# A planner that treats the ports shared by VectorE and GpSimd as an exclusive lock, in a decay-attention and MoE kernel

## The chip, the cores and the metric

The kernel runs on one core of a Trainium2 chip. The core has five engines, each working through its own instructions in a fixed order: TensorE (PE, matmuls), VectorE (DVE), ScalarE (ACT), GpSimd (POOL) and SyncE (SP, which here issues all DMAs). An instruction waits at the head of its engine's queue until what it needs is done, and what stands behind it waits as well. The metric is the device time of one execution in microseconds (us), as the median over several runs.

## The reference

Eight batches of eight heads, 576 positions, head size 64, all in float32. The causal attention has a decay from the running sum of log f, and its output, with the heads side by side, goes through two matmuls with a piecewise function between them.

```python
def _attn_ref(q, k, v, f):
    B, H, S, D = q.shape                                  # 8, 8, 576, 64
    scores = np.matmul(q, k.transpose(0, 1, 3, 2)) / np.sqrt(D)
    cum = np.cumsum(np.log(np.clip(f, 0.0001, 1.0)), axis=-1)
    decay = cum[:, :, :, None] - cum[:, :, None, :]
    scores = np.where(causal, -1000000000.0, scores + decay)
    attn = np.exp(scores - np.max(scores, axis=-1, keepdims=True))
    attn = attn / (np.sum(attn, axis=-1, keepdims=True) + 1e-09)
    return np.matmul(attn, v)

def _moe_ref(x, w_in, w_out):                             # x: 4608 x 512
    h = x @ w_in                                          # 512 x 2048
    g = np.where(h >= 1, h, np.where(h <= -1, 0.0, (h + 1) ** 2 / 4))
    return g @ w_out                                      # 2048 x 512
```

## The kernel before

**The work.** Two heads make a pair; 36 jobs (`jobs`, the first batch is cut into rows 0 to 255 and the rest) run over the pairs. A job has row blocks of 128 rows. For each block, `scores` puts the scores into PSUM with PE (L831), POOL makes the decay row in SBUF (tensor_scalar, L837, and the causal affine_select, L841), and `weights` lets DVE subtract the two with the row minimum on the way (L923, one input in PSUM, one in SBUF), ACT take the exponential and its sum (L927), and DVE the reciprocal (L935, L938). From the sixth job on, float32 values are carried as two float16 parts: ACT writes the high part (L941), DVE the rest as value minus high part (scalar_tensor_tensor with both tensors in SBUF, L947; for some blocks of two jobs POOL does it, L945), and a transposing DMA puts them the other way round (L953). The first five jobs stay in float32 and are transposed by PE against a diagonal that ACT writes (`turn_rows`, L852, L863). `values` multiplies with V (L968, results by L977 and L978). `prepare` splits and transposes Q and K of the next job (L745, L747, one buffer `qs`; in the first twelve jobs they stay in float32 and PE transposes them, L709 to L718), `measure` takes their norms, `split_values` splits V (L794, L795), `value_max` reads V for its largest value (L544). Decay rows lie in a ring of four buffers (`sdr`) and one of two (`sd4`).

**The MoE.** Tokens are taken in chunks of 256 and the hidden columns in eight blocks of 256; one chunk with one block is a unit. `moe_front` multiplies into the PSUM tile `ph` (two buffers, L1012), ACT writes relu(u) and its square (L1021, L1022), DVE chooses between them (L1023, one input in PSUM), ACT writes the high half of g (L1025) and DVE the low half (L1026, both inputs in SBUF). `moe_back`, two units later, multiplies g with the second weights (L1041) and empties the sums (L1054, L1058). The weights, too, are split into two float16 parts at the beginning, by `weight_split`: three integer steps on DVE (L495, L498, L501), squares on ACT (L505), a scale (`from_norms`, L409 to L418), the high part on ACT (L509), and the low part on POOL (L511, L512) or DVE (L514). `moe_scales` derives each batch's small factors (L579 to L604).

**The order.** The program is first written in one order. Then `plan` (the last line of the kernel) rearranges it: `traced` makes a `Step` of every instruction, with what it must follow, a duration from `Step.cost` (times `SLOW`, except on PE) and a rank, which is its place in the program plus `SHIFT` for the function and engine that it comes from. `arranged` then plays the steps through in time. For each engine it takes, among the steps that are ready, one that can begin within `LOOK` = 50 ns of the engine's becoming free, the lowest rank first, and otherwise the one that can begin first; the engine whose choice begins earliest goes next. It models rings of buffers, DMA queues, a PE clock that halves after a quiet window, and the overlap of successive instructions. The order found is pinned on every engine. The hardware keeps that order and takes its own time. In `arranged` before, DVE and POOL know nothing of each other but their data.

The constants before:

```python
SLOW = 1.03
LOOK = 50
SHIFT = {("from_norms", "PE"): -100, ("measure", "DVE"): 400, ("moe_back", "DVE"): 200,
         ("moe_back", "SP"): 800, ("split_values", "ACT"): 1500, ("turn_rows", "ACT"): -25,
         ("value_max", "DVE"): -100, ("weight_split", "DVE"): 200, ("weights", "POOL"): 400}
```

Of the kernel before, what the change touches and what calls it, by code (L numbers as in the profile page):

```python
# [49 lines left out]
RING = 1500  # L50
SLOW = 1.03
LOOK = 50
SHIFT = {
    ("from_norms", "PE"): -100,
    ("measure", "DVE"): 400,
    ("moe_back", "DVE"): 200,
    ("moe_back", "SP"): 800,
    ("split_values", "ACT"): 1500,
    ("turn_rows", "ACT"): -25,
    ("value_max", "DVE"): -100,  # L60
    ("weight_split", "DVE"): 200,
    ("weights", "POOL"): 400,
}

# [27 lines left out]
class Step:  # L92


    def __init__(self, k, ins):
        self.k, self.ins, self.engine = k, ins, ENGINES[ins.engine.name]
        self.reads, self.writes = ([self.part(a) for a in args if hasattr(a, "bass_ap")] for args in (ins.ins, ins.outs))
        self.after, self.waits, self.tiles = set(), [], set()

    @staticmethod  # L100
# [17 lines left out]
    def cost(self):  # L118
        e, out = self.engine, self.writes[0]
        n = out[4]  # L120
# [11 lines left out]
        if e == "ACT":  # L132
            return 150 + (0.82 if wide and wide[0][0][:2] in ("s_", "ph", "po") else 0.93) * n + 100 * min(len(self.reads) - 1 + len(self.writes) - 1, 3)
        if e == "POOL":
            if self.ins.opcode == "TensorTensor":
                return 450 + 2.0 * n
            return 260 + 0.95 * n if "Affine" in self.ins.opcode else 460 + 1.15 * n
        if wide:
            n = max(n, wide[0][4])
        fast = len(wide) == 1 and self.ins.opcode == "TensorScalarPtr"  # L140
        return 170 + 55 * (scalars > 0) + (0.6 if fast else 1.08) * n + (20 if len(self.writes) > 1 else 0)

# [66 lines left out]
def arranged(steps, users, order, rings):  # L209
# [15 lines left out]
    ready = {e: {} for e in LATE}  # L225
    chains = {e: [] for e in LATE}
    fly, dma, warm, border, busy, form = [], 0.0, False, WINDOW, 0.0, None
    for s in steps:
        if not s.open:
            ready[s.engine][s.k] = 0  # L230
    for _ in steps:
        best = None
        for e, cands in ready.items():
            pick = None
            for k, t in cands.items():
# [10 lines left out]
                else:  # L246
                    begin = max(t, free[e])
                    c = (free[e] if begin <= free[e] + LOOK else begin, s.rank, begin, k)
                    if pick is None or c < pick:
# [45 lines left out]
        else:  # L295
            end = t + s.time
            free[e] = end - OVERLAP[e]
        s.end = end + LATE[e]
# [923 lines left out]
```

## Time and profile before

| | |
|---|---|
| median of 3 runs | 1062.35 us (1059.92 to 1063.02) |
| the profiled execution, its own time | 1060.71 us |
| its span, first to last instruction | 1058.9 us |
| mean granted PE clock | 0.973 |
| busy: PE, DVE, ACT, POOL | 1003.1, 793.0, 786.9, 435.4 us |
| packets' time of the DMA queue, share of 16 engines' span | 61.0% |

Busy time is the union of an engine's instructions. A DVE or POOL instruction that has been started and stands still counts as busy. The granted clock is 1 when PE runs at its full clock. A line such as L1026 is a line of the kernel file; names such as g<-u,z say what is written from what.

### The profile page before, as it was taken

To read this page: it belongs to the slowest core of one execution; us is meant where nothing else is said; L and a number is where in the kernel's file an instruction comes from. 1 tells how busy PE (TensorE), PEld (TensorE's weight loads), DVE (VectorE), ACT (ScalarE), POOL (GpSimd) and SP (SyncE) were. 2 spreads that over 40 slices of the span, in tenths; PEclk is the share of its full clock that TensorE was granted. 3 is DMA by queue.
4 is the path that set the end of the run, shared out by engine and by line. 5 is a ranking of instruction groups with operands and counts; after the bars stand their busy time and mean duration, and the time that the engine had idled before them with its cause. 6 is when DMAs were issued, how large, how long until landed. Compare 5 with 4: busy or idle time off the path is not lost.

```text
span 1058.9 us, 24420 instructions
## 1 busy us (share of the span) xinstructions
PE 1003.1 (95%) x8859; PEld 657.7 (62%) x8859; DVE 793.0 (75%) x2095; ACT 786.9 (74%) x1634; POOL 435.4 (41%) x677
## 2 busy tenths in 40 slices
PE   3769888799999999999999999999999999999998
PEld 2546555366666676667666666666666666677665
DVE  5999999999998878977776677887788866322222
ACT  3788888788888878886776688888888877344443
POOL 2887776736443544442332344454445441000000
PEclk9869899889999999999999999999999999999999
DMA  9967669789997777785455476767676654000000
GB/s 298 305 203 206 167 163 194 182 169 187 198 189 184 175 167 151 170 185 128 119 128 131 81 175 144 158 150 160 147 161 143 142 104 95 3 22 19 3 20 20
DMA packets 406041, 152.18 MB, mean 144 GB/s; under 512 B 379680, under 2 KB 382752, under 8 KB 405920
## 3 DMA queue, kind: packets, MB, share of 16 engines
q1 hardware_dynamic: 405920, 150.62, 61.0%
q8 instruction: 69, 1.13, 0.5%
q14 instruction: 52, 0.43, 0.1%
HBM read 75.64 MB, written 9.58 MB: 80 GB/s over the span
## 4 chain that ended last, share of the span: by engine, by line
PE 56%; DMA 0%; DVE 0%; issue 0%; ACT 0%; DVEq 0%
PE ph L1012 25%; PE po L1041 24%; PE s L831 4%; PE s L968 3%; DMA vst<-in_v_dram 0%; DVE pr L947 0%; PE ph L409 0%; DVE u L1023 0%; PE ph L401 0%; DVE x L978 0%; ACT ot L1058 0%; PE ph L397 0%; ACT u L1022 0%; DVE sdr L923 0%; DVE rc L938 0%
## 5 line engine op out<-in xcount | busy, mean ns | idle before, releaser
L1012 PE MATMUL ph<-x,place 128*128 128x256 f16 (+3 forms) x4608 | 413.1, 247 | 1.2 <-DVE u L1023 0.7
L1041 PE MATMUL po<-place,g 128*128 128x512 f16 x1728 | 403.5, 381 | 2.3 <-ACT g L1025 1.0
L1012 PEld LDWEIGHTS <-place 128*128 128x128 f16 x4608 | 353.2, 99 | 61.9 <-issue 21.3
L1041 PEld LDWEIGHTS <-g 128*128 128x128 f16 x1728 | 165.9, 98 | 180.6 <-issue 8.0
L837 POOL TENSOR_SCALAR sdr<-ck,nsig,cqs 128x128 f32<-128x128 f32 (+1 forms) x192 | 150.1, 789 | 269.3 <-DVE pr L947 258.1
L1023 DVE SCALAR_TENSOR_TENSOR u<-ph,z,u 128x512 f32<-128x512 f32 x128 | 95.6, 747 | 128.5 <-ACT u L1022 128.3
L1021 ACT ACTIVATE u<-ph,z 128x512 f32<-128x512 f32 x128 | 98.8, 772 | 117.3 <-PE ph L1012 116.9
L927 ACT ACTIVATE sdr<-sdr,nm 128x384 f32<-128x384 f32 (+1 forms) x248 | 137.3, 555 | 24.7 <-DVE nm L923 22.2
L947 DVE SCALAR_TENSOR_TENSOR pr<-sdr,rc,pr 128x384 f16<-128x384 f32 (+2 forms) x232 | 126.7, 584 | 8.0 <-ACT pr L941 6.6
L1025 ACT ACTIVATE g<-u,z 128x512 f16<-128x512 f32 x128 | 91.8, 717 | 51.7 <-DVE u L1023 50.9
L1026 DVE SCALAR_TENSOR_TENSOR g<-u,z,g 128x512 f16<-128x512 f32 x128 | 98.2, 767 | 41.0 <-ACT g L1025 40.5
L941 ACT ACTIVATE pr<-sdr,rc 128x384 f16<-128x384 f32 (+1 forms) x236 | 118.7, 556 | 7.3 <-issue 2.8
L831 PE MATMUL s<-qkT 64*64 64x512 f16 (+11 forms) x1056 | 111.4, 336 | 6.0 <-DVE nm L923 2.9
L923 DVE CUSTOM_DVE_ANT_0 sdr<-s,sdr,nalpha 128x128 f32<-128x128 f32 (+1 forms) x192 | 99.0, 544 | 13.1 <-PE s L831 7.4
L841 POOL TENSOR_SCALAR_AFFINE_SELECT sdr<-sdr 128x128 f32<-128x128 f32 x248 | 97.7, 414 | 2.3
L837 POOL TENSOR_SCALAR sd<-ck,nsig,cqs 64x576 f32<-64x576 f32 x48 | 51.1, 1064 | 115.1 <-DMA ck<-cum_d 46.7
L1022 ACT ACTIVATE u<-u 128x512 f32<-128x512 f32 x144 | 89.7, 623 | 1.9
L968 PE MATMUL s<-pT,vs 128*64 128x320 f16 (+3 forms) x1098 | 69.8, 279 | 3.2 <-DVE nm L923 3.2
L968 PEld LDWEIGHTS <-vs 128*64 128x64 f16 x1098 | 48.6, 110 | 27.0 <-issue 9.3
L831 PEld LDWEIGHTS <-qkT 64*128 64x128 f16 (+1 forms) x864 | 32.4, 98 | 44.0 <-issue 29.4
L747 DVE SCALAR_TENSOR_TENSOR qs<-qk,sc,qs 128x640 f16<-128x640 f32 x48 | 45.6, 962 | 5.3 <-ACT qs L745 4.4
L837 POOL TENSOR_SCALAR sdr<-ck,cq 128x384 f32<-128x384 f32 (+3 forms) x48 | 40.4, 842 | 17.1 <-DVE pr L947 12.6
(157 smaller groups left out, 1027.7 us busy)
## 6 DMA issues: line engine op xcount, KB each, us to landing
ck<-cum_d SPq DMA_DIRECT2D x64, 288.0 KB, 4.0
out_dram<-ot SPq DMA_DIRECT2D x36, 256.0 KB, 2.2
qk<-in_k_dram SPq DMA_DIRECT2D x68, 128.0 KB, 2.7
vst<-in_v_dram SPq DMA_DIRECT2D x28, 288.0 KB, 3.4
v<-in_v_dram SPq DMA_DIRECT2D x62, 128.0 KB, 2.8
qk<-in_q_dram SPq DMA_DIRECT2D x60, 128.0 KB, 2.9
place<-in_moe_w_in_dram SPq DMA_DIRECT2D x6, 1024.0 KB, 6.9
place<-in_moe_w_out_dram SPq DMA_DIRECT2D x5, 1024.0 KB, 7.8
```

The costliest lines, as they stand in the source:

```text
L831: nc.tensor.matmul(sds[h % len(sds)][1][p0:p1, c0:c1], lhsT=a[rows, q0 - w.s0:q0 - w.s0 + p1 - p0], rhs=b[rows, c0:c1], start=(i == 0), st ...
L837: nc.gpsimd.tensor_scalar(out=sd[p0:p1, 0:wid], in0=w.ck[h][p0:p1, 0:wid], scalar1=w.nsig if w.p < NQK else w.nsig[p0:p1], scalar2=w.cqs[p ...
L841: nc.gpsimd.affine_select(sd[p0:p1, q0:wid], sd[p0:p1, q0:wid], pattern=[[-1, wid - q0]], channel_multiplier=1, base=0, compare_op=ALU.is_ ...
L923: nc.vector.tensor_tensor_reduce(out=a, in0=sp[:, 0:wid], in1=a, scale=w.nalpha, scalar=BIG, op0=ALU.add, op1=ALU.min, accum_out=nm[:, i:i ...
L927: nc.scalar.activation(a, a, AF.Exp, bias=nm[:, i:i + 1], scale=-1.0, accum_out=sm[:, i:i + 1])
L941: nc.scalar.activation(pr[:, :, 0, i, :], a, AF.Copy, scale=rc[:, i:i + 1])
L947: nc.vector.scalar_tensor_tensor(out=pr[:, :, 1, i, :], in0=a, scalar=rc[:, i:i + 1], in1=pr[:, :, 0, i, :], op0=ALU.mult, op1=ALU.subtract,)
L968: nc.tensor.matmul(av[64 * h:64 * h + 64, at + s0:at + s1], lhsT=w.vs[:, vl, h, t, :], rhs=w.pT[:, t, pl, h, s0:s1], start=(t == 0 and pi ...
L1012: nc.tensor.matmul(ph[:, fi, a0:a1], lhsT=wi[fb][:, wl, t, fi * P:(fi + 1) * P], rhs=xs[b][:, t, xl, s0:s0 + a1 - a0], start=(fi == 0 and ...
L1021: nc.scalar.activation(u, h, AF.Relu, scale=z.u[:, i:i + 1], bias=z.h[:, i:i + 1])
L1026: nc.vector.scalar_tensor_tensor(out=g[:, 1], in0=u, scalar=z.r[:, i:i + 1], in1=g[:, 0], op0=ALU.mult, op1=ALU.subtract)
L1041: nc.tensor.matmul(po[ch][i], lhsT=g[:, gl, fi * TC + i * P:fi * TC + (i + 1) * P], rhs=wo[fb][:, wl, fi, :], start=(first and fi == 0 and ...
```

## The change

Only the planner changes; the instructions and their data are the same, and their order on the engines is what it finds.

- `Step` has a new mark `shares`: DVE instructions of the kinds tensor_scalar, scalar_tensor_tensor and tensor_tensor that write more than one element per partition and whose first input isn't one of the PSUM tiles (`s_`, `ph`, `po`).
- `arranged` keeps `hold`, the end of the last such DVE step, and `pool`, the end of the last POOL step. A sharing DVE step may not begin earlier than `pool` - 140 ns, a POOL step not earlier than `hold` - 100 ns, and if one still begins ahead of that end, its own end is moved behind it.
- The formulas for durations of ACT, POOL and DVE steps get new constants, ACT no longer tells PSUM inputs from SBUF ones, and `SLOW` goes from 1.03 to 1.01.
- `SHIFT` is a new table: ("turn_rows", "ACT") and ("moe_back", "DVE") leave it, eight entries come in, and that of ("value_max", "DVE") is changed.

```diff
@@ -48,18 +48,26 @@
 ENGINES = {"PE": "PE", "DVE": "DVE", "Activation": "ACT", "Pool": "POOL", "SP": "SP"}
 WINDOW = 3413.3
 RING = 1500
-SLOW = 1.03
+SLOW = 1.01
+AWARE = True
 LOOK = 50
 SHIFT = {
+    ("across", "PE"): 50,
+    ("from_norms", "DVE"): -25,
     ("from_norms", "PE"): -100,
     ("measure", "DVE"): 400,
-    ("moe_back", "DVE"): 200,
+    ("moe_back", "ACT"): -1500,
     ("moe_back", "SP"): 800,
+    ("moe_front", "ACT"): -1500,
+    ("moe_scales", "DVE"): 25,
+    ("prepare", "DVE"): -1500,
     ("split_values", "ACT"): 1500,
-    ("turn_rows", "ACT"): -25,
-    ("value_max", "DVE"): -100,
+    ("turn_rows", "PE"): 50,
+    ("value_max", "DVE"): -25,
     ("weight_split", "DVE"): 200,
+    ("weights", "DVE"): 25,
     ("weights", "POOL"): 400,
+    ("weights", "SP"): 50,
 }
 
 
@@ -96,6 +104,10 @@
         self.k, self.ins, self.engine = k, ins, ENGINES[ins.engine.name]
         self.reads, self.writes = ([self.part(a) for a in args if hasattr(a, "bass_ap")] for args in (ins.ins, ins.outs))
         self.after, self.waits, self.tiles = set(), [], set()
+        self.shares = (
+            self.engine == "DVE" and ins.opcode in ("TensorScalarPtr", "TensorTensor")
+            and self.writes[0][4] > 1 and self.reads[0][0][:2] not in ("s_", "ph", "po")
+        )
 
     @staticmethod
     def part(a):
@@ -130,15 +142,15 @@
                 return max(1340, 1.17 * n)
             return 430 if n > 500 else 620
         if e == "ACT":
-            return 150 + (0.82 if wide and wide[0][0][:2] in ("s_", "ph", "po") else 0.93) * n + 100 * min(len(self.reads) - 1 + len(self.writes) - 1, 3)
+            return 190 + 0.845 * n + 92 * min(len(self.reads) - 1 + len(self.writes) - 1, 3)
         if e == "POOL":
             if self.ins.opcode == "TensorTensor":
-                return 450 + 2.0 * n
-            return 260 + 0.95 * n if "Affine" in self.ins.opcode else 460 + 1.15 * n
+                return 185 + 1.89 * n
+            return 177 + 0.86 * n if "Affine" in self.ins.opcode else 322 + 0.83 * n
         if wide:
             n = max(n, wide[0][4])
         fast = len(wide) == 1 and self.ins.opcode == "TensorScalarPtr"
-        return 170 + 55 * (scalars > 0) + (0.6 if fast else 1.08) * n + (20 if len(self.writes) > 1 else 0)
+        return 147 + 62 * (scalars > 0) + (0.52 if fast else 1.04) * n
 
 
 def clash(a, b):
@@ -224,6 +236,7 @@
     free = {e: 400 for e in LATE}
     ready = {e: {} for e in LATE}
     chains = {e: [] for e in LATE}
+    hold = pool = 0
     fly, dma, warm, border, busy, form = [], 0.0, False, WINDOW, 0.0, None
     for s in steps:
         if not s.open:
@@ -245,6 +258,10 @@
                         t = max(t, gone[queue[base][j]])
                 else:
                     begin = max(t, free[e])
+                    if AWARE and s.shares:
+                        begin = max(begin, pool - 140)
+                    elif AWARE and e == "POOL":
+                        begin = max(begin, hold - 100)
                     c = (free[e] if begin <= free[e] + LOOK else begin, s.rank, begin, k)
                     if pick is None or c < pick:
                         pick = c
@@ -294,6 +311,14 @@
             free[e] = end
         else:
             end = t + s.time
+            if e == "POOL":
+                if hold > t:
+                    end = max(end, hold + s.time - 100)
+                pool = end
+            elif s.shares:
+                if pool > t:
+                    end = max(end, pool + max(s.time - 140, 24))
+                hold = end
             free[e] = end - OVERLAP[e]
         s.end = end + LATE[e]
         for name in s.tiles:
```

## The prediction

> **What bounds the kernel now.** I read the page first, then the busy times by stretch, then PE's waits, then the groups of VectorE (DVE) in the stretch that the first views pointed to.
>
> ```profile
> PE 1003.1 (95%) x8859; PEld 657.7 (62%) x8859; DVE 793.0 (75%) x2095; ACT 786.9 (74%) x1634; POOL 435.4 (41%) x677
> PE   3769888799999999999999999999999999999998
> DVE  5999999999998878977776677887788866322222
> POOL 2887776736443544442332344454445441000000
> PEclk9869899889999999999999999999999999999999
> ```
>
> PE is busy 95% of the span, yet its first eight or nine slices are not full, and in just those DVE reads 9 in every slice but the first and POOL reads 7 to 8 in most. From the tenth slice on (about 240 us) PE is full to the end. The busy times by stretch give the sizes; the columns are the stretch, its length, then busy time of PE, PEld, DVE, ACT and POOL, the granted PE clock, the DMA share and GB/s.
>
> ```profile
> 0.00:80.00 80.00, 46.09 (x255) 33.49 (x256) 64.25 (x146) 49.89 (x114) 52.33 (x72) 0.81 0.85 269
> 80.00:106.00 26.00, 25.95 (x186) 15.61 (x186) 24.72 (x56) 22.50 (x45) 20.09 (x25) 0.98 0.75 203
> 106.00:159.00 53.00, 46.48 (x328) 28.16 (x325) 51.42 (x128) 46.23 (x93) 40.32 (x50) 0.94 0.68 165
> 159.00:212.00 53.00, 43.62 (x287) 22.40 (x285) 50.26 (x149) 42.84 (x97) 37.08 (x52) 0.90 0.86 187
> 212.00:240.00 28.00, 26.42 (x200) 17.04 (x201) 25.48 (x79) 24.27 (x52) 10.03 (x17) 0.88 0.86 177
> 240.00:901.00 661.00, 660.28 (x6358) 435.70 (x6356) 533.30 (x1485) 535.76 (x1143) 275.57 (x466) 1.00 0.69 151
> 901.00:1058.90 157.90, 154.24 (x1260) 105.28 (x1260) 43.57 (x58) 65.46 (x94) 0.00 (x0) 1.00 0.04 14
> ```
>
> From 240 to 901 us PE is idle 0.72 us at full clock, after that 3.66 us, which is the tail behind the last matmul. No order of the same work can win there; a poor one can lose. PE's idle time lies ahead of it: 80.00 - 46.09 = 33.9 us in the first 80 us, then 0.05 + 6.52 + 9.38 + 1.58 = 17.5 us up to 240 us. The clock is the second loss: the granted share below 1, times the stretch, is 15.2 us before 80 us and 26 x 0.02 + 53 x 0.06 + 53 x 0.10 + 28 x 0.12 = 12.4 us from 80 to 240 us, both upper bounds, since a slow clock costs nothing while PE idles. So the prize is at most 30 us between 80 and 240 us, and at most 49 us before it. As PE is full from 240 us on, a microsecond won ahead of it is a microsecond off the end.
>
> Who holds PE up there? PE's waits, in total us, times and the longest; the first row is from 0 to 80 us, the others from 80 to 240 us.
>
> ```profile
> PE ph L863 <- ACT pr L852: 22.7, 8, 9.5
> ...
> PE s L714 <- DVE rc L935: 3.3, 1, 3.3
> PE s L968 <- DVE nm L923: 3.2, 2, 1.7
> PE s L831 <- DVE nm L923: 2.9, 3, 1.5
> ...
> PE po L1041 <- ACT g L1025: 1.0, 1, 1.0
> PE po L1041 <- DVE g L1026: 0.9, 2, 0.5
> ```
>
> Early on PE waits for the diagonals of the first pairs (L852), which stand behind the chain of decay (POOL), subtraction (DVE) and exponential (ACT); later mostly for DVE. From 80 to 212 us DVE is busy 24.72 + 51.42 + 50.26 = 126.4 of 132 us, 96%, ACT 111.6, 85%. DVE is the nearest bound. But part of its busy time is waiting. The timelines of DVE (first two rows) and of POOL (last two) around 171 us, start, duration, operation:
>
> ```profile
> 170.80 1.88 DVE L1026 SCALAR_TENSOR_TENSOR g<-u,early_z,g 128x512 f16<-128x512 f32 x1
> 172.60 0.74 DVE L923 CUSTOM_DVE_ANT_0 sd<-s,sd 128x576 f32<-128x576 f32 x1
> ...
> 169.98 2.15 POOL L512 TENSOR_TENSOR place<-x,place 128x1024 f16<-128x1024 f32 x1
> 172.08 0.75 POOL L841 TENSOR_SCALAR_AFFINE_SELECT sdr<-sdr 128x128 f32<-128x128 f32 x1
> ```
>
> DVE's step with both tensors in SBUF began 0.8 us into POOL's, and ended 0.55 us after POOL did; POOL's next select then lasted until DVE was through. One engine at a time: while POOL holds, this DVE step stands, and everything queued behind it on DVE with it.
>
> **The change, part by part.** All of it is in the planner that fixes the order on each engine before the kernel is built; no instruction is added or removed.
>
> *The lock in the plan.* It now starts a sharing DVE step no earlier than 140 ns before POOL's end (and POOL 100 ns before DVE's); as a step that can begin within 50 ns beats one that can't, DVE is then given a step that reads PSUM or a reduction in the meantime. What it can win is the waiting inside DVE's rows. Groups of DVE from 26.5 to 212 us, count, busy us and mean ns; the last row is from the part after 901 us, where POOL does nothing.
>
> ```profile
> L1026 DVE SCALAR_TENSOR_TENSOR g<-u,early_z,g 128x512 f16<-128x512 f32 x11 | 13.8, 1256 | 0.0
> L501 DVE SCALAR_TENSOR_TENSOR place<-place,qs 128x1024 int32<-128x1024 int32 x9 | 12.8, 1421 | 0.1
> L514 DVE SCALAR_TENSOR_TENSOR place<-place,sw 128x1024 f16<-128x1024 f32 x5 | 8.1, 1611 | 0.8 <-ACT place L509 0.8
> L501 DVE SCALAR_TENSOR_TENSOR x<-x,qs 128x1024 int32<-128x1024 int32 x5 | 6.4, 1279 | 0.0
> L935 DVE TENSOR_SCALAR rc<-sm 128x2 f32<-128x2 f32 x20 | 6.4, 318 | 1.5 <-ACT sdr L927 1.5
> L930 DVE TENSOR_SCALAR rc<-sm 128x2 f32<-128x2 f32 x9 | 3.4, 374 | 0.9 <-ACT sdr L927 0.8
> L514 DVE SCALAR_TENSOR_TENSOR place<-x,sw,place 128x1024 f16<-128x1024 f32 x2 | 2.5, 1264 | 0.0
> L603 DVE TENSOR_SCALAR early_z<-early_z 128x4 f32<-128x4 f32 x1 | 2.3, 2257 | 0.0
> L583 DVE TENSOR_SCALAR z<-z 128x8 int32<-128x8 int32 x1 | 2.1, 2089 | 0.0
> L935 DVE TENSOR_SCALAR rc<-sm 128x1 f32<-128x1 f32 x6 | 0.8, 140 | 0.1
> ...
> L1026 DVE SCALAR_TENSOR_TENSOR g<-u,z,g 128x512 f16<-128x512 f32 x29 | 21.8, 751 | 22.9 <-ACT g L1025 22.9
> ```
>
> Each against its undisturbed like: L1026 11 x (1256 - 751) = 5.6 us; L935 20 x (318 - 140) = 3.6; L930 9 x (374 - 140) = 2.1; L501 9 x (1421 - 1279) = 1.3; L514 5 x (1611 - 1264) = 1.7; the single L603 and L583, against the 140 ns of a tiny step, 2.1 and 1.9. Together 18.3 us in which DVE stood although it counts as busy. A second is won only where DVE has something else to do: work that doesn't need the shared ports. From 80 to 212 us:
>
> ```profile
> L923 DVE CUSTOM_DVE_ANT_0 sdr<-s,sdr 128x384 f32<-128x384 f32 (+3 forms) x42 | 20.6, 507 | 1.4 <-PE s L831 1.4
> L1023 DVE SCALAR_TENSOR_TENSOR u<-ph,early_z,u 128x512 f32<-128x512 f32 x11 | 8.1, 740 | 1.1 <-ACT u L1022 1.1
> L544 DVE TENSOR_REDUCE m<-vst 128x1 f32<-128x576 f32 x8 | 5.9, 741 | 0.4 <-DMA vst<-in_v_dram 0.4
> L923 DVE CUSTOM_DVE_ANT_0 sd<-s,sd 128x576 f32<-128x576 f32 x6 | 4.5, 749 | 0.0
> L923 DVE DVE_READ_ACCUMULATOR2_ANT nm<- 128x1 f32 x48 | 3.8, 79 | 0.0
> ```
>
> 42.9 us of DVE's 126.4, 34%. I let that third of the stalls be filled: 18.3 x 0.34 = 6.2 us. The bounds are 0 (nothing ready at those moments) and 18.3 (all). I stay near the lower end, as L923 itself needs a decay row that POOL has just made and scores from PE.
>
> *Durations fitted anew.* For L1026 the plan said (170 + 55 + 1.08 x 512) x 1.03 = 801 ns, and now (147 + 62 + 1.04 x 512) x 1.01 = 749, the undisturbed row's 751. Not all come closer: ACT's 128x512 read out of PSUM (L1021, below) was planned at 793 and is now 815, against 765. Better in one place, worse in another: zero. The bounds are one of PE's listed waits either way, -3.3 to +3.3 us.
>
> *Ranks.* Steps of 50 or less move only ties: zero, within the same bound. Three move far, by 1500 places: the ACT work of both MoE halves, and DVE's part of the preparation, always win now against attention on their engine. ACT from 80 to 212 us, and the preparation over the whole run:
>
> ```profile
> L1021 ACT ACTIVATE u<-ph,early_z 128x512 f32<-128x512 f32 x11 | 8.4, 765 | 0.7 <-PE ph L1012 0.7
> L747 DVE SCALAR_TENSOR_TENSOR qs<-qk,sc,qs 128x640 f16<-128x640 f32 x48 | 45.6, 962 | 5.3 <-ACT qs L745 4.4
> ```
>
> Ahead of 212 us there are 11 units. An exponential that finds such a step ahead of it loses at most one, 11 x 0.765 = 8.4 us if every one falls on the path; in return the two PE waits for g, 1.9 us, may go. I take zero, because ACT is idle 15% of that stretch and PE's long waits there name DVE; -1.9 and +8.4 are kept for the range. The preparation's two steps cost 2 x 0.962 = 1.9 us to a pair, once, as its target is a single buffer: zero, with 1.9 as a bound; of 48 only a few fall ahead of 240 us. SP's rank of +50 lets a weights transpose stand behind a load or two; the loads run ahead of need, except that L968 waited twice, 3.2 us, already inside the bound.
>
> *The clock.* If PE's gaps of 17.5 us shrink by 6.2, up to the same 35% of the 12.4 us may go with them, 4.4 us; one slow stretch more, at the price of the worst one, costs 53 x 0.10 = 5.3. I take zero: which windows turn slow depends on how the gaps fall.
>
> *After 240 us.* PE's cover there is DVE's slack (533 of 661 us busy). Where it fails, PE loses what its waits show ahead, 1 to 3 us a time; I take zero.
>
> **The sum.** The profiled execution took 1060.71 us, 1.64 under the median of 1062.35 and 1.8 over its span. 1060.7 - 6.2 = 1054.5; on the footing of the median 1056.1, so I say 1056. What a measurement of this kernel can tell from no change is about 0.3%, 3.2 us.
>
> **The rivals.** *The lock is full.* From 80 to 212 us POOL alone is busy 20.09 + 40.32 + 37.08 = 97.5 of 132 us, and DVE's sharing steps fill most of the 126.4 - 42.9 = 83.5 us left of its own: 181 us of holding and waiting in 132. If what remains after the waits is still close to 132, the two engines' holds follow each other without a gap, and no order makes them shorter: a DVE step placed under a hold only makes DVE idle later, when it comes to its turn. Then the result is 1062, give or take 3. For it: that sum. Against it: DVE has its 34% outside the lock, and POOL's idle 34.5 us there are not all DVE's holds. The Trainium skill says the same in its page "SBUF — State Buffer", section "Who interferes with whom": the shared pair is an exclusive lock, held for the whole instruction, and the issue order decides who blocks. By that rule the sum of holds is a floor under the stretch, and the time would be this rival's 1062; the trace agrees on the lock (1.88 us in place of 0.75), and leaves open whether the floor is reached.
>
> *MoE first starves attention.* The -1500 on ACT puts relu, square and the output ahead of exponentials, the next rows of weights and with them the second batch's tokens come later, and PE's continuous stretch starts later than 212 to 240 us. Price: up to the 8.4 us above, less a third of the forecast gain, 2: 1062.35 + 6.4 = 1068.7. It decides once more than about 8 of 11 units push an exponential of the path, as 8 x 0.765 cancels the 6.2. For it: ACT at 85%, and PE's largest early wait, 22.7 us, being one for ACT. Against it: MoE is also what PE has to do there.
>
> *Much more.* If two thirds of the stalls go and the clock follows, 12.2 + 4.4 = 16.6: 1046.
>
> **How the numbers follow.** The forecast (a gain of 3.2 to 11 us) gets 0.43, the large gain 0.12, the full lock 0.25, the starved attention 0.20. That makes faster 0.55, same 0.25, slower 0.20. The range: down to 1046, the large gain's own value, which leaves out about 0.06; up to 1066, past the full lock's 1065.5, which leaves out most of the slower cases, 0.14.
>
> **What would show it.** Right: in the groups of DVE from 26.5 to 212 us, L1026 under 1000 ns and L935 under 250; PE's idle from 80 to 240 us at 11 to 13 us, against 17.5; PE without gaps from some 6 us earlier; after that unchanged. The full lock: those means fall, but DVE's idle grows by the same amount and PE's gaps stay. The starved attention: PE waits for ACT behind L1021 to L1025, and the last gap of PE lies after 240 us. Wrong altogether would be a change of more than 2 us after 240 us, or in the first 30 us.

## The result, and the profile after

The changed kernel takes 1070.99 us (median of 4 runs, 1067.1 to 1072.28) against 1061.68 us before (4 runs, 1059.92 to 1063.02): the ratio is 1.0087, with a 95% interval of 1.0072 to 1.0102. It is slower by 0.87%, 9.2 us. The forecast of 1056 was wrong, and the range up to 1066 didn't hold the time. The profiled execution took 1070.31 us, its span is 1068.5 us, and the mean granted PE clock is 0.979, against 0.973. Ratios, here and below, are of undisturbed executions alone; the only other one is one of the ten of `e13_after_free_max`, which took 5683.69 us.

The page of the kernel after: first the busy times, then the rows of the 40 slices that were shown of before.

```profile
PE 1003.2 (94%) x8859; PEld 657.5 (62%) x8859; DVE 772.0 (72%) x2095; ACT 789.1 (74%) x1634; POOL 437.3 (41%) x677
...
PE   3679798879999999999999999999999999999998
...
DVE  5879888999888877986676778887788776222222
...
POOL 3687765744554443552321435445444541000000
PEclk9969899989999999999999999999999999999999
```

PE's work is the same to 0.1 us. DVE is busy 21 us less, and of the first ten slices, of which all but the first read 9 before, five now read 7 or 8: DVE stands waiting less, but it is idle in place of it. The busy times of the kernel after by stretch show where the 9.6 us of span were lost; the columns are as before (stretch, length, busy PE, PEld, DVE, ACT, POOL, clock, DMA share, GB/s).

```profile
0.00:80.00 80.00, 47.81 (x248) 33.28 (x250) 57.58 (x147) 49.29 (x112) 47.05 (x67) 0.86 0.82 252
80.00:106.00 26.00, 24.07 (x166) 14.59 (x163) 24.41 (x54) 20.08 (x43) 19.42 (x29) 0.96 0.92 266
106.00:159.00 53.00, 43.83 (x293) 25.17 (x292) 44.71 (x118) 41.51 (x82) 39.05 (x42) 0.90 0.74 178
159.00:212.00 53.00, 44.55 (x338) 26.25 (x332) 46.12 (x136) 46.28 (x102) 33.88 (x50) 0.97 0.77 179
212.00:240.00 28.00, 19.99 (x153) 12.11 (x153) 26.44 (x88) 21.16 (x46) 14.28 (x24) 0.88 0.99 208
240.00:901.00 661.00, 659.11 (x6355) 434.86 (x6354) 524.49 (x1496) 539.97 (x1154) 283.62 (x468) 1.00 0.66 146
901.00:1068.50 167.50, 163.83 (x1325) 111.27 (x1322) 48.30 (x65) 70.79 (x102) 0.00 (x0) 1.00 0.08 23
```

PE's busy time against before: +1.7 us in the first 80, -10.0 us from 80 to 240, -1.2 us from 240 to 901. Together that is -9.5 us, the difference of the spans to 0.1 us; PE does this work after 901 us, in a stretch that is 9.6 us longer. So the loss lies in the very stretch in which the gain was forecast: PE is idle there for 27.6 us against 17.5. DVE's busy time in the same stretch fell from 151.9 to 141.7 us (24.41 + 44.71 + 46.12 + 26.44), its idle time rose from 8.1 to 18.3. In a stretch of fixed length the one follows from the other; what it tells is that the time freed was, in sum, not filled with other work.

PE's waits of the kernel after, 80 to 240 us (total us, times, longest):

```profile
PE s L856 <- DVE nm L948: 8.2, 6, 4.6
PE ph L434 <- ACT place L530: 5.1, 3, 4.3
PE s L739 <- DVE x L1003: 3.1, 3, 1.6
PE ph L434 <- ACT qs L753: 3.0, 2, 1.6
...
PE po L1066 <- ACT g L1050: 1.4, 2, 1.1
```

Lines stand 25 later than before, so L856 is L831, L948 is L923. PE waits for the same operation as before, DVE's subtraction with the row minimum, but for 8.2 us in place of 2.9. DVE's own waits of the kernel after, 80 to 260 us, the longest two:

```profile
DVE m L569 <- DMA vst<-in_v_dram: 7.3, 5, 2.3
DVE g L1051 <- ACT g L1050: 1.8, 3, 0.9
```

In front of five instructions of L569 (`value_max`, the reduction of V to its largest value; L544 before) DVE was idle for 7.3 us, because their load hadn't landed. Before it was 0.4 us, once.

### The profile page after: what moved, and what is told of

It is laid out like the page before. It is cut to its first block, busy times and chain, and to the rows that moved or that the text cites. A ratio compares the mean times of both kernels' runs of the same rounds, so it can differ in the third digit from the quotient of the medians.

```text
span 1068.5 us, 24424 instructions
## 1 busy us (share of the span) xinstructions
PE 1003.2 (94%) x8859; PEld 657.5 (62%) x8859; DVE 772.0 (72%) x2095; ACT 789.1 (74%) x1634; POOL 437.3 (41%) x677
## 4 chain that ended last, share of the span: by engine, by line
PE 70%; DVE 1%; issue 1%; DMA 0%; POOL 0%; ACT 0%; SPq 0%; DVEq 0%; POOLq 0%
PE ph L1037 30%; PE po L1066 30%; PE s L856 5%; PE s L993 5%; DMA vst<-in_v_dram 0%; PE ph L434 0%; DVE g L1051 0%; DVE qs L772 0%; PE ph L426 0%; DVE pr L972 0%; POOL sdr L862 0%; DVE x L1003 0%; DVE u L1048 0%; POOL sdr L866 0%; ACT ot L1083 0%
## 5 line engine op out<-in xcount | busy, mean ns | idle before, releaser
L862 POOL TENSOR_SCALAR sdr<-ck,nsig,cqs 128x128 f32<-128x128 f32 (+1 forms) x192 | 144.0, 753 | 251.8 <-DVE pr L972 216.1
L972 DVE SCALAR_TENSOR_TENSOR pr<-sdr,rc,pr 128x384 f16<-128x384 f32 (+2 forms) x232 | 130.7, 586 | 21.7 <-ACT pr L966 20.2
L966 ACT ACTIVATE pr<-sdr,rc 128x384 f16<-128x384 f32 (+1 forms) x236 | 123.4, 556 | 13.9 <-issue 7.2
L856 PE MATMUL s<-qkT 64*64 64x512 f16 (+11 forms) x1056 | 114.2, 340 | 12.4 <-DVE nm L948 8.6
L1051 DVE SCALAR_TENSOR_TENSOR g<-u,z,g 128x512 f16<-128x512 f32 x128 | 98.7, 771 | 34.8 <-ACT g L1050 34.7
L866 POOL TENSOR_SCALAR_AFFINE_SELECT sdr<-sdr 128x128 f32<-128x128 f32 x248 | 110.6, 457 | 9.3
L948 DVE CUSTOM_DVE_ANT_0 sdr<-s,sdr,nalpha 128x128 f32<-128x128 f32 (+1 forms) x192 | 99.7, 543 | 12.4 <-PE s L856 11.8
L862 POOL TENSOR_SCALAR sd<-ck,nsig,cqs 64x576 f32<-64x576 f32 x48 | 49.9, 1040 | 118.0 <-DMA ck<-cum_d 45.3
L856 PEld LDWEIGHTS <-qkT 64*128 64x128 f16 (+1 forms) x864 | 32.8, 98 | 44.4 <-issue 31.2
L862 POOL TENSOR_SCALAR sdr<-ck,cq 128x384 f32<-128x384 f32 (+3 forms) x48 | 37.5, 782 | 33.5 <-DVE pr L972 26.5
L952 ACT ACTIVATION_READ_ACCUMULATOR sdr<-sdr,nm 128x1 f32 x248 | 46.8, 189 | 0.0
```

The source lines that it names most:

```text
L856: nc.tensor.matmul(sds[h % len(sds)][1][p0:p1, c0:c1], lhsT=a[rows, q0 - w.s0:q0 - w.s0 + p1 - p0], rhs=b[rows, c0:c1], start=(i == 0), st ...
L862: nc.gpsimd.tensor_scalar(out=sd[p0:p1, 0:wid], in0=w.ck[h][p0:p1, 0:wid], scalar1=w.nsig if w.p < NQK else w.nsig[p0:p1], scalar2=w.cqs[p ...
L866: nc.gpsimd.affine_select(sd[p0:p1, q0:wid], sd[p0:p1, q0:wid], pattern=[[-1, wid - q0]], channel_multiplier=1, base=0, compare_op=ALU.is_ ...
L948: nc.vector.tensor_tensor_reduce(out=a, in0=sp[:, 0:wid], in1=a, scale=w.nalpha, scalar=BIG, op0=ALU.add, op1=ALU.min, accum_out=nm[:, i:i ...
L952: nc.scalar.activation(a, a, AF.Exp, bias=nm[:, i:i + 1], scale=-1.0, accum_out=sm[:, i:i + 1])
L966: nc.scalar.activation(pr[:, :, 0, i, :], a, AF.Copy, scale=rc[:, i:i + 1])
```

## The experiments

Three theories stood after the first look (R, D and O); T came with the second round of runs, and F out of the traces later.

- **R**: the new ranks (MoE's ACT steps 1500 places up) starve the attention.
- **D**: the new durations make a worse plan.
- **O**: the plan charges too much for the lock, and so gives up good order to avoid it.
- **T**: the table of ranks before had been fitted to that one plan; any other plan of the same work loses some 7 to 12 us, in many places at once.
- **F**: `value_max`, which POOL doesn't hold up (its 17 instructions of the kernel after from 80 to 260 us lasted 724 to 753 ns), is taken as a filler under POOL's holds long before it is needed, and costs DVE time and waits in the stretch where DVE is the bound.

Each ratio is against the kernel before, run alongside.

### Parts of the change alone

`e1_no_lock`: the change without the lock (new durations, new ranks).

```diff
-AWARE = True
+AWARE = False
```

> The changed kernel with the lock left out of the plan; new durations and new ranks stay. Theory O (the plan prices the lock far above what it costs, and buys its avoidance with a worse order): the loss goes, 1057 to 1064 us. Theory R (the new ranks, MoE first on ScalarE, starve attention): as slow as the changed kernel, 1068 to 1073. Theory D (the new durations mislead the plan): 1068 to 1073 as well.

Measured: 1080.12 us, ratio 1.0187 (1.0169 to 1.0205).

`e2_old_ranks`: the change with the table `SHIFT` of before; the far ranks of its diff:

```diff
-    ("moe_back", "ACT"): -1500,
+    ("moe_back", "DVE"): 200,
...
-    ("moe_front", "ACT"): -1500,
-    ("moe_scales", "DVE"): 25,
-    ("prepare", "DVE"): -1500,
...
```

> The changed kernel with the ranks of before; lock and new durations stay. Theory O: slow, 1068 to 1077 us, since this plan's own end is 6 us later than that of the changed kernel (1061.9 against 1055.6 us by its own clock). Theory R: back to before, 1059 to 1064. Theory D: slow, 1068 to 1073.

Measured: 1072.35 us, ratio 1.0115 (1.0093 to 1.0137).

`e3_durations_alone`: the kernel before with the new constants in `cost` and `SLOW` = 1.01; no lock, old ranks. Two of the lines, against the kernel before:

```diff
-SLOW = 1.03
+SLOW = 1.01
...
-        return 170 + 55 * (scalars > 0) + (0.6 if fast else 1.08) * n + (20 if len(self.writes) > 1 else 0)
+        return 147 + 62 * (scalars > 0) + (0.52 if fast else 1.04) * n
```

> The kernel before with the new durations alone: no lock, old ranks. Theory O: no loss, 1055 to 1063 us. Theory R: no loss either. Theory D: the loss is here already, 1068 to 1073.

Measured: 1075.3 us, ratio 1.0138 (1.012 to 1.0157).

The new durations alone cost 1.4%. The new ranks cost 0.5% more where the lock is left out (e1 against e3) and win a little or nothing where it is in (1.0087 against 1.0115): putting the old ranks back does not bring the time back. The lock wins back 1.0% with the new ranks (e1 against the change) and about 0.2% with the old (e3 against e2), inside the intervals. The whole change is therefore better than its parts, and yet worse than before. D looked like the answer here. `e4_small_steps_free`, the change with DVE steps of 16 elements or fewer freed from the lock in the plan, has no time, as the order found for it deadlocks: whether the price of the small steps is what misleads the plan stays untested.

### Two constants that mean nothing

`e8_look40` and `e11_slow_101`: the kernel before, with one constant of the plan moved a little.

```diff
-LOOK = 50
+LOOK = 40
```

> The kernel before with one constant of its plan moved that says nothing of the chip: LOOK 40 in place of 50 ns. Theory T (the ranks before fit this one plan, and any other plan with them loses): 1066 to 1073 us. Rival (the old plan is good as such, small changes of its constants do not matter): 1058 to 1064.

Measured: 1068.53 us, ratio 1.0081 (1.0066 to 1.0097).

```diff
-SLOW = 1.03
+SLOW = 1.01
```

> The kernel before with SLOW 1.01 in place of 1.03 alone, which makes all planned durations off TensorE 2% shorter. Theory T: 1064 to 1071 us. Rival (only a change of what the plan knows of the lock or of single kinds of steps matters): 1058 to 1063.

Measured: 1071.01 us, ratio 1.0091 (1.0072 to 1.011).

No lock, no refitted duration, no changed rank, and the loss is that of the whole change. That takes the ground from D as a theory of its own: a scaling of the durations without any refit already costs 0.9%. It is what T expects. It also limits what the runs above can tell: between two plans, a difference of under 1% need not come from the part in which they were meant to differ, and that holds for R and for the lock's 1.0% too. The busy times from 80 to 240 us, first before, then e11:

```profile
80.00:240.00 160.00, 142.46 (x992) 83.20 (x991) 151.89 (x408) 135.83 (x285) 107.52 (x141) 0.92 0.78 181
```

```profile
80.00:240.00 160.00, 133.55 (x933) 78.73 (x930) 147.16 (x395) 129.63 (x267) 103.29 (x140) 0.91 0.71 173
```

PE loses 8.9 us there, as with the change.

### A POOL that reads less, in three fixed orders

For these three the planner's choice is written into the kernel step for step, so that nothing is planned anew. These runs were meant to take away most of what holds DVE up: POOL's tensor_scalar (L837) becomes a memset of the same extent, which reads nothing, and the select reads `ck`. The decay and with it the sums are left out.

```diff
-            nc.gpsimd.tensor_scalar(
-                out=sd[p0:p1, 0:wid], in0=w.ck[h][p0:p1, 0:wid], scalar1=w.nsig if w.p < NQK else w.nsig[p0:p1],
-                scalar2=w.cqs[p0:p1, r, h:h + 1], op0=ALU.mult, op1=ALU.add,
-            )
+            nc.gpsimd.memset(sd[p0:p1, 0:wid], 0.0)
             nc.gpsimd.affine_select(
-                sd[p0:p1, q0:wid], sd[p0:p1, q0:wid],
+                sd[p0:p1, q0:wid], w.ck[h][p0:p1, q0:wid],
...
```

> The order of the kernel before, kept step for step, but POOL's decay rows are only set to zero (a memset of the same extent, about as long, which reads nothing), and the causal select reads the decay row instead: decay and sums are left out, and with POOL's reads most of the contention for the ports. What the time falls by is what the lock costs in this order. Theory O (the order before paid little for the lock): 1052 to 1058 us. Theory T (the lock plays no part in the differences; the order before is simply a lucky one among many): also a small fall.

Measured: 1054.11 us, ratio 0.9945 (0.993 to 0.996).

> The same replacement in the order of the changed kernel. Theory O (this order has bought its freedom from collisions with a worse order of everything else): hardly any fall, 1066 to 1071 us, so 10 to 15 over the order before with the same replacement. Rival (the lock still costs more here than before): a fall to 1060 or less.

Measured: 1070.27 us, ratio 1.0089 (1.0066 to 1.0113).

> The same replacement in the order of the run with the new durations alone. Theory O (that order loses by collisions that its plan does not know of): a fall of some 20 us, to 1050 to 1058. Theory T: as far above the order before as with the lock, 1068 to 1073.

Measured: 1066.15 us, ratio 1.0059 (1.0039 to 1.0079).

The replacement takes 0.55%, 5.8 us, off the order before, nothing that can be measured off the changed order (1.0087 without it, 1.0089 with it), and 0.8% off e3's order (1.0138 and 1.0059). That is not the cost of the lock, because most of the stalls are still there. Groups of DVE in e5, 26.5 to 212 us (L1106 is L1026 of the kernel before, L584 is L501, L597 is L514, L1015 and L1010 are L935 and L930):

```profile
L1106 DVE SCALAR_TENSOR_TENSOR g<-u,early_z,g 128x512 f16<-128x512 f32 x11 | 10.7, 970 | 0.0
L584 DVE SCALAR_TENSOR_TENSOR x<-x,qs 128x1024 int32<-128x1024 int32 x5 | 9.4, 1875 | 0.0
...
L597 DVE SCALAR_TENSOR_TENSOR place<-place,sw 128x1024 f16<-128x1024 f32 x5 | 7.9, 1582 | 1.0 <-ACT place L592 1.0
...
L1015 DVE TENSOR_SCALAR rc<-sm 128x2 f32<-128x2 f32 x21 | 6.3, 300 | 1.9 <-ACT sdr L1007 1.9
...
L1010 DVE TENSOR_SCALAR rc<-sm 128x2 f32<-128x2 f32 x9 | 6.1, 679 | 0.9 <-ACT sdr L1007 0.8
```

Against the prediction's undisturbed values these are 2.4, 3.0, 1.6, 3.4 and 4.9 us, together 15.3, where the prediction counted 18.3 before. Over all rows of DVE steps with SBUF inputs, each against the shortest mean of its kind and shape in any run, an estimate gives some 30 us before and 23 in e5. POOL itself has much less to do: 81.2 us busy from 80 to 240 us in e5, 107.5 before. How much of the 5.8 us comes from the 3 to 7 us of stalls that went and how much from POOL's shorter work is open, and so is the cost of the whole lock. In the changed order POOL's busy time there falls from 106.6 to 74.8 us, DVE's from 141.7 to 140.1, and the time stays. A bound by the sum of the two engines' times would have sunk by 33 us, so this order is not held by it. With the same replacement the changed order is 1.0089 / 0.9945 = 1.45%, 15 us, longer than the order before. The stretch from 80 to 240 us, e5 and then e6:

```profile
80.00:240.00 160.00, 146.28 (x1049) 86.88 (x1049) 148.22 (x424) 140.73 (x298) 81.23 (x149) 0.94 0.81 191
```

```profile
80.00:240.00 160.00, 130.84 (x937) 78.23 (x938) 140.06 (x390) 128.79 (x267) 74.80 (x141) 0.93 0.84 201
```

PE is busy 15.4 us less in e6, with DVE idle for 19.9 us in place of 11.8.

### A cheaper lock

In `e9_soft_lock` no step is held back; a step that meets the other engine's hold is only lengthened in the plan.

```diff
-                    if AWARE and s.shares:
-                        begin = max(begin, pool - 140)
-                    elif AWARE and e == "POOL":
-                        begin = max(begin, hold - 100)
...
-                if hold > t:
-                    end = max(end, hold + s.time - 100)
+                if hold > t + 100:
+                    end += 0.8 * (hold - 100 - t)
...
-                if pool > t:
-                    end = max(end, pool + max(s.time - 140, 24))
+                if pool > t + 140:
+                    end += 0.3 * (pool - 140 - t)
```

> The changed kernel with a cheaper lock in its plan: no step is held back, a POOL step is lengthened by 0.8 of what is left of a sharing VectorE step, a VectorE step by 0.3 of what is left of POOL's; durations and ranks as changed. Theory O (the plan prices the lock too high): 1060 to 1066 us, faster than the changed kernel's 1071. Theory T (the ranks before fit one plan, and any other plan loses): 1066 to 1075.

Measured: 1072.26 us, ratio 1.0106 (1.0084 to 1.0128).

`e10_soft_lock_old_ranks`: the same with the table `SHIFT` of before, as in e2.

> The same cheaper lock and the new durations, with the ranks of before. Theory O: 1055 to 1062 us, so as fast as the kernel before, since with a lock at its price the new durations do no harm. Theory T: 1066 to 1075, like every other plan that these ranks were not fitted to.

Measured: 1067.86 us, ratio 1.007 (1.0047 to 1.0093).

`e12_searched`: the cheaper lock, with `LOOK` = 20, `SLOW` = 1.05 and some 30 ranks found by a search over the plan with this lock, of which the diff shows those of `value_max` and of POOL's part of `weights`.

```diff
-SLOW = 1.01
-LOOK = 50
+SLOW = 1.05
+LOOK = 20
...
-    ("value_max", "DVE"): -25,
+    ("value_max", "DVE"): 800,
...
-    ("weights", "POOL"): 400,
+    ("weights", "POOL"): 1500,
```

> The cheaper lock with ranks searched anew for it, some 30 entries (SLOW 1.05, LOOK 20). If a plan with the lock at its price foretells the chip: 1047 to 1056 us, faster than both kernels. If the ranks only fit the plan and not the chip: 1058 to 1068.

Measured: 1063.07 us, ratio 1.0018 (1.0003 to 1.0033).

The price alone doesn't do it: O explains at most 0.4% with the old ranks (1.007 against e2's 1.0115), nothing with the new ones. Ranks fitted to the new plan bring the time to within 0.2% of the kernel before, and no further. No version of these runs beats the kernel before with its computation whole.

### The filler

The tile of `value_max` shows what the changed order does differently, 80 to 260 us. Before:

```profile
L544 DVE TENSOR_REDUCE m<-vst x9: 727/743/753, 88.4 to 239.0; 128x1 f32<-128x576 f32 x9
```

After:

```profile
L569 DVE TENSOR_REDUCE m<-vst x17: 724/742/753, 86.6 to 256.9; 128x1 f32<-128x576 f32 x17
```

The columns are the count, the duration in ns and the first and last start. Eight more of them in the crowded stretch, 5.9 us of DVE, for batches that come long after. One of them, the 14th of 28 (the order before runs its 14th after 300 us), stands in the timelines of the kernel after at 156 us (start, duration, in brackets the idle time before it and what ended it), DVE:

```profile
152.75 1.23 DVE L523 SCALAR_TENSOR_TENSOR qs<-place,qs 128x1024 int32<-128x1024 int32 x1
156.29 0.75 DVE L569 TENSOR_REDUCE m<-vst 128x1 f32<-128x576 f32 x1 [2.30 <-DMA vst<-in_v_dram]
156.96 0.68 DVE L948 CUSTOM_DVE_ANT_0 sdr<-s,sdr 128x512 f32<-128x512 f32 x1
```

The engines that wait for what stands behind it, POOL, ACT and PE:

```profile
155.00 0.29 POOL L866 TENSOR_SCALAR_AFFINE_SELECT sdr<-sdr 128x128 f32<-128x128 f32 x1
```

```profile
157.74 0.72 ACT L952 ACTIVATE sdr<-sdr,nm 128x512 f32<-128x512 f32 x1 [4.17 <-DVE rc L960]
```

```profile
158.45 1.75 PE L993 MATMUL s<-pT,vs 128*64 128x320 f16 x30 [1.50 <-DVE nm L948]
```

POOL had finished its decay rows by 155.29. DVE stood from 153.98 to 156.29 for a load that nobody needed yet, with the subtraction L948 queued behind it; ACT was idle for 4.17 us and PE for 1.50, of which this place doesn't show how much the load caused. To learn what all of these cost, both orders were again fixed step for step, with the reduction of the later batches made free: it reads 8 elements of a constant and waits for no load (their scales come out of that constant).

```diff
-            out=vmax[b][:, i:i + 1], in_=vpart[0] if b else vparts[i], axis=AX.X, op=ALU.max, apply_absolute_value=True
+            out=vmax[b][:, i:i + 1], in_=ones[:, 0:8] if b else vparts[i], axis=AX.X, op=ALU.max, apply_absolute_value=True
```

> The changed kernel's order, step for step, with one reduction made free: the reading of V for its largest value in the batches after the first (128x576, 0.742 us) reads 8 elements of a constant instead, so it takes little and waits for no load. The scales of those batches come out of that constant, which the output shows; nothing else is left out. In the changed kernel 17 of these lie between 80 and 260 us, with 7.3 us of idle time of VectorE in front of five of them; before there were 9, with 0.4 us. Theory F (these reductions, taken as fillers under GpSimd's holds long before they are needed, are what VectorE loses): 17 x 0.6 + 7.3 = 17.5 us go from VectorE, against 9 x 0.6 + 0.4 = 5.8 in the order before; the time falls to 1055 to 1061, and stands less than 3 us over the same thing done to the order before. Theory T (any order that the ranks were not fitted to loses in many places at once): it gains no more than the order before does, 1066 to 1070, and stays 7 to 11 us above it.

Measured: 1061.83 us, ratio 1.0009 (1.0 to 1.0019).

> The mirror of it: the order before, step for step, with the same reduction made free (the same scales are wrong). Both theories: 9 x 0.6 + 0.4 = 5.8 us go from VectorE between 80 and 260 us, of which some part reaches the end: 1056 to 1061. What tells the theories apart is the distance to the run on the changed order: under 3 us for F, 7 to 11 us for T.

Measured: 1057.87 us, ratio 0.9976 (0.9966 to 0.9986).

In `e15_after_short_max` the reduction is as short, but reads the tile that the load fills, and so still waits for it.

```diff
-            out=vmax[b][:, i:i + 1], in_=vpart[0] if b else vparts[i], axis=AX.X, op=ALU.max, apply_absolute_value=True
+            out=vmax[b][:, i:i + 1], in_=vpart[0][:, 0:8] if b else vparts[i], axis=AX.X, op=ALU.max, apply_absolute_value=True
```

> The changed kernel's order with the reduction cut to 8 elements of the tile that it read before, so that it still waits for its load but takes little itself (the maxima, and the scales of the later batches, are those of 8 elements). It parts the two halves of theory F: if the busy time counts, 17 x 0.6 = 10.2 us less on VectorE, 1060 to 1066; if the wait for the load counts instead, it stays within 3 us of the changed kernel, 1068 to 1072, while the run that also doesn't wait falls. Theory T: 1067 to 1071.

Measured: 1067.31 us, ratio 1.0058 (1.0042 to 1.0075).

The changed order gains 0.78% (8.3 us) from the free reduction, the order before 0.24% (2.5 us). The distance between the orders falls from 0.87% to 1.0009 / 0.9976 = 0.33%: 5.7 of the 9.2 us are the reductions, and 3.5 us (with the two intervals, 2 to 5) are something else. F's limit of 3 us is missed by a little, T's 7 to 11 clearly. Of the changed order's 8.3 us the busy time is 0.29% (3.1 us, e15), and the waits for the loads, which only e13 removes, are 0.49% (5.2 us); in e15 these waits add up to 9.9 us from 80 to 260 us, against 7.3 in the kernel after, presumably as DVE comes to its loads sooner. The stretch from 80 to 240 us in e13 and in e14:

```profile
80.00:240.00 160.00, 136.07 (x990) 81.92 (x989) 142.90 (x417) 135.40 (x282) 106.43 (x142) 0.94 0.87 200
```

```profile
80.00:240.00 160.00, 142.78 (x1012) 83.84 (x1012) 149.94 (x414) 139.46 (x294) 112.03 (x148) 0.95 0.82 185
```

In the changed order PE rises from 132.4 us to 136.1, in the order before from 142.5 to 142.8. So 3.6 of the 8.3 us show as busy time of PE in this stretch; PE also does more in that time, 990 matmuls against 940.

`e16_loads_held` tries it in the planner: a load of `value_max` isn't offered while it lies over 1600 steps ahead of the program's first unplaced step.

```diff
+AHEAD = 1600
+SWAPS = [(1063, 1084), (1084, 1086)]
...
+            s.early = kinds.get(ins.name) == "value_load"
...
+        while front in placed:
+            front += 1
...
+                if s.early and k > front + AHEAD:
+                    continue
```

> The changed planner with one rule more: a load of V for the largest value isn't offered while its place in the program is over 1600 steps ahead of the first step not yet placed (in the order before, these loads lie at most 1600 steps ahead; in the changed one up to 6000). Two steps of VectorE are also kept in the program's order, so that the order can run. The rest is planned anew. Nothing of the computation is left out. Theory F alone: the reductions and their waits leave the stretch up to 260 us, and what the run with the free reductions gained over the order before, 5.7 us, comes back: 1063 to 1067. Theory T: the rule changes hundreds of later choices, so that the gain is overlaid by whatever the new order happens to cost, anything from 1062 to 1074, while the number of these reductions in the stretch falls all the same to 8 to 10.

Measured: 1069.89 us, ratio 1.0073 (1.0052 to 1.0093). Its tile from 80 to 260 us, DVE's first wait there, and the busy times from 80 to 240 us:

```profile
L580 DVE TENSOR_REDUCE m<-vst x8: 728/748/753, 85.2 to 223.1; 128x1 f32<-128x576 f32 x8
```

```profile
DVE m L580 <- DMA vst<-in_v_dram: 5.4, 4, 3.1
```

```profile
80.00:240.00 160.00, 136.94 (x962) 80.94 (x959) 142.19 (x385) 130.32 (x268) 102.53 (x141) 0.91 0.74 180
```

The count falls from 17 to 8, below that of before, but DVE still waits 5.4 us for the loads of four of them, and the time is the changed kernel's within the intervals. As the rule changes the rest of the order too, the run doesn't tell what the far ones alone cost. A plan in which the reduction comes only when its load has landed on the chip, and not only in the plan, wasn't tried.

## Why the prediction was wrong

**What bounds the kernel** was read rightly. The stretch from 80 to 240 us decides, and a microsecond lost there is lost at the end: PE's -10.0 us there, with +1.7 and -1.2 on either side, are the whole of the result. The sign that would have been "wrong altogether" (over 2 us after 240 us) didn't appear, the tail is 3.67 us against 3.66.

**The stalls** were sized rightly for the rows that were listed, and went as the lock in the plan meant them to. (The sum leaves out L417 before, seven 128x2 steps of 479 ns, which take 160 in the kernel after: 2.2 us more.) Groups of DVE after, 26.5 to 212 us (count, busy us, mean ns):

```profile
L569 DVE TENSOR_REDUCE m<-vst 128x1 f32<-128x576 f32 x19 | 14.1, 742 | 7.5 <-DMA vst<-in_v_dram 7.3
...
L526 DVE SCALAR_TENSOR_TENSOR place<-place,qs 128x1024 int32<-128x1024 int32 x9 | 11.1, 1234 | 0.0
...
L1051 DVE SCALAR_TENSOR_TENSOR g<-u,early_z,g 128x512 f16<-128x512 f32 x11 | 9.3, 844 | 1.8 <-ACT g L1050 1.8
...
L539 DVE SCALAR_TENSOR_TENSOR place<-place,sw 128x1024 f16<-128x1024 f32 x5 | 7.8, 1564 | 3.3 <-ACT place L534 3.3
...
L955 DVE TENSOR_SCALAR rc<-sm 128x2 f32<-128x2 f32 x9 | 4.2, 480 | 0.0
...
L960 DVE TENSOR_SCALAR rc<-sm 128x2 f32<-128x2 f32 x18 | 3.6, 197 | 1.5 <-ACT sdr L952 1.4
...
L612 DVE TENSOR_SCALAR early_z<-early_z 128x4 f32<-128x4 f32 x1 | 1.0, 1040 | 0.0
L612 DVE TENSOR_SCALAR early_z<-early_z 128x2 f32<-128x2 f32 x1 | 0.9, 947 | 0.0
...
L605 DVE TENSOR_SCALAR early_z<-early_z 128x4 int32<-128x4 int32 x1 | 0.9, 896 | 0.0
```

Both signs named came true: L1026, now L1051, fell from 1256 to 844 ns, and L935, now L960, from 318 to 197. The prediction's sum of 18.3 us, done again against the same undisturbed values, is 11 x 0.093 + 18 x 0.057 + 9 x 0.340 + 5 x 0.300 = 6.6 us, and the three single steps of a few elements (against 140 ns) add 2.5: 9.1 us, half of it gone. L526 (L501 before) has none left, L955 (L930 before) got worse. What the stalls that went were worth at the end by themselves, no run shows; together with the order that avoids them they came out at a loss of 9.2 us where 6.2 us of gain stood.

**The step that failed** is in "The lock in the plan": "DVE is then given a step that reads PSUM or a reduction in the meantime", and a third of the stalls counted as filled, with the filling counted as gain. The list of work outside the lock held the very row, L544 with 5.9 us, and that row was counted without asking for when its result is needed. A filler that isn't due gives nothing back before 240 us; it takes 0.742 us each time, and where it waits for its own load it blocks DVE's queue as the lock did. The working asked how much of DVE's work is outside the lock, when the question was how much of it is on the path. The first row above, 7.5 us of idle time in front of L569, is that wait: 5.2 us of the end by e13 and e15, later waits of the same kind included. With their busy time the reductions make 5.7 of the 9.2 us by which the orders differ.

The second omission is in the same part: "Durations fitted anew" and "Ranks" were priced at zero, with bounds of 3.3 and 8.4 us, as if what a plan doesn't intend to change stayed where it was. But every choice changes those after it. Two constants without any meaning for the hardware moved the time by 0.8 and 0.9%, as much as the whole change. That term should have stood in the sum with a price, and its sign could be argued from the table: ranks like -25 or 50 look like what a search leaves behind. (The new table takes in nine entries, not eight. And the 3.2 us that "Ranks" put down to a late transposing DMA are, in the row of L968, waits that DVE's subtraction ended.)

**The rivals.** *MoE first starves attention* gave 1068.7, near the result, for a reason that the runs don't bear out: with the old ranks the time is no better (1072.35), and PE's waits after name DVE's subtraction and the weights' squares (L530) far ahead of g (1.4 us). *The lock is full* had its first two signs, shorter means and more idle time of DVE, but PE's gaps didn't stay, they grew by 10 us, and its reason fails for the changed order: with 33 us less of POOL and DVE in the stretch nothing was gained (e6). The page "SBUF — State Buffer" of the Trainium skill, section "Who interferes with whom", calls the pair an exclusive lock held for the whole instruction; the traces agree for single instructions (1.88 us in place of 0.75), but e6 shows that the sum isn't what bounds this stretch in the changed order. *Much more* needed gaps of PE that shrink; they grew.

**What stays open.** 3.5 of the 9.2 us between the orders aren't tied to a place. That they are the price of any other plan (T) fits e8, e11 and e12, but is an argument and not a measurement, as each of these orders loses in a different place. F is shown for the changed order alone. From 80 to 260 us e2, the other order from a plan with the full lock, has 16 of these reductions with 8.7 us of waits for their loads; without that lock e1 has 14 with 0.3 us, e3 9 with none, e11 12 with 0.2 and e8 10 with 3.1. So e3's 1.4% and most of e11's 0.9% were lost elsewhere.

## What to carry to other kernels

Work that is put under a stall is a gain only if it is due: ask of each filler when its result is read, and whether it can itself wait with the critical instruction queued behind it. A planner that prefers anything that can start now over what is needed next should know when each result is due; that is advice, no run here shows it, and e16, which limits these loads by their place in the program, gained nothing. And a list of priorities tuned against one cost model belongs to that model: before crediting a better model with its effect, move a constant that means nothing and see how much the time moves by itself.

## What the runs showed of the hardware

DVE's stalls don't go when POOL's largest group of instructions stops reading. In e5, with the decay's tensor_scalar as a memset, the rows shown above still hold 15.3 us from 26.5 to 212 us, and one group, the 128x1024 steps of L584 on `x`, is longer than before (1875 ns in place of 1279).

A step of a few elements waits like a large one: the 128x2 steps of L955 took 480 ns on average, single 128x4 steps 1040 ns (L612) and, in the kernel before, 2257 ns (L603). The 128x1 form of L960 shows no such wait in its six instances. Its row of the kernel after, 26.5 to 212 us:

```profile
L960 DVE TENSOR_SCALAR rc<-sm 128x1 f32<-128x1 f32 x6 | 0.8, 140 | 0.0
```
